# A spectral filter and a sine feed-forward layer on one core: the first batch's backward table, its filter rows and the idle products

## The chip, the core and the metric

The kernel runs on one core of a Trainium2 chip. The core has a matrix engine (TensorE, PE in the profile), a vector engine (VectorE, DVE), a scalar engine (ScalarE, ACT), GpSimd (POOL) and a sync engine (SyncE, SP) that only starts transfers. Each engine works through its own list of instructions in order and waits for the others by semaphores. Transfers between main memory and the on-chip memory run on 16 DMA engines; they are started from the queues of SP, ACT and POOL. TensorE writes its products to PSUM, and VectorE or ScalarE copy them from there to the on-chip memory SBUF. The metric is the time of one execution in microseconds (us) as the device reports it; smaller is better.

## The reference, cut to what matters

```python
batch, seq, dim = (8, 3008, 256)          # d_ff = 2048

def _attn_ref(x, filt_r, filt_i):
    X = np.fft.rfft(x, axis=1)
    F = (filt_r + 1j * filt_i)[None, :, :]
    return np.fft.irfft(X * F, n=x.shape[1], axis=1).astype(np.float32)

def _moe_ref(x, w_in, w_out, alpha):       # x: all 8 * 3008 rows of the above
    h = x @ w_in
    s = np.sin(alpha * h)
    g = h + s * s / (alpha + 1e-09)
    return (g @ w_out).astype(np.float32)
```

Each of 8 batches of 3008 rows of 256 channels goes through a Fourier transform along the rows, a product with a filter per frequency and channel, and the transform back. Then every row goes through a layer of 2048 hidden units with the activation h + sin(alpha h)^2 / alpha.

## The kernel before

**The transform.** 3008 is written as 64 times 47, and 47 x 64 as a two-step transform: a short one of length 47 (24 frequencies are kept, tables `wa`, `wa2` forward and `we`, `we2` backward) and one of length 64 for each of the 24 (tables `wb` forward and `wg` backward, each 128 x 3072 in float16, 786 KB). A tile `xs` holds, for four of the 24, the 128 rows of a spectrum: rows 0 to 63 real parts, 64 to 127 imaginary parts. The filter lies in `fri` (128 x 2 x 24 x 256, real and imaginary plane); its rows 64 to 127 repeat rows 0 to 63, the imaginary plane with its sign changed.

**Batches 1 to 7** store intermediate tiles in main memory and load them back turned (`shuffle1`, `shuffle2`). Their product with the filter (`product`, four VectorE instructions) exchanges the two halves of rows on the way, and one TensorE product with `wg` follows (`f2g`).

**Batch 0** is worked with no such trip. `load_x(0, 4)` loads it in four parts. `f1_chip(k)`, k = 0 to 7, is the short transform (two groups of 4 products, one copied out by ScalarE, one by VectorE, into `a_c`). `turn1(t)`, t = 0 to 11, turns `a_c` by products with the identity into `bint`. `f2x(0, t)` is the long forward transform into `xs`. `product(0, k, 0)` makes z = xs * real filter and t = xs * imaginary filter (the last two on VectorE, 128x1024 each), with no exchange of rows; the exchange is put into a second backward table, `wgs`, which is `wg` with its halves of rows exchanged, so that `g_chip(k, half)` adds two products, z with `wg` and t with `wgs`. `b_c` collects them, `turn2(j)` turns them into `gin[0]` (4 of the 16 turns ahead of the layer, 12 within it), and `f3(G, cb)` is the short transform back into `yt`, the rows that the layer reads. `psf`, the PSUM ring that `turn2` and `f3` share, has three tiles; so has `psh`, which `f1_chip`, `turn1`, `keep_busy` and the layer's first product share; `pso` has two.

Before the change `wgs` is made on the chip: `swap_wg` copies the halves of `wg` (four VectorE copies in all). `fold_filter(s0, n)` fills rows 64 to 127 of `fri` for eight of the 24 frequencies: a VectorE copy for the real plane and a multiplication by -1 for the imaginary one (ScalarE for the first eight, VectorE for the rest). `keep_busy(n, src)` issues n products of 128x512 that nobody reads.

**The layer** goes in 47 groups of 512 rows (index g), each in 8 slots (q): `mlp_in` (two products and one sine on ScalarE, twice a slot), `square` on VectorE every second slot, and `mlp_out` of the group before. A table `plan`, filled by `at(slot, function, ...)`, puts all other work into slot 8g + q: the transforms of the next batch, `prep_w_out` (w_out scaled into `w_out2`), `cast_w_out` (on GpSimd), `prep_w_inT` and `prep_m` (a 256x256 product of the two weights), `prep_w_ina` (w_in times alpha). The program is written under `tc.manual_schedule()`: the order of the instructions on each engine is the order in which the functions are called.

**Queues.** SP carries the tables: `wb` (first 8 frequencies), `wg` (first 8), `wb` (rest), `wg` (rest), then the first half of `w_out`. POOL carries x (batch 0), the filter in twelve transfers, `w_in`, x of batch 1, the second half of `w_out`, `alpha_b` and `w_in32`. `gate` makes a transfer wait for an earlier one to land. The tile pools hand a buffer on when its last reader is done: `wgs` lies in the pool of `vt` before the change.

Of the kernel before, what the change touches and what calls it, by code (L numbers as in the profile page):

```python
# [9 lines left out]
FP16 = mybir.dt.float16  # L10
FP32 = mybir.dt.float32
AFT = mybir.ActivationFunctionType
ALU = mybir.AluOpType

B, S, C, DFF = 8, 3008, 256, 2048
MT, R, NK, RP = 47, 64, 24, 32
# [3 lines left out]
def dft_tables():  # L20

    m = np.arange(MT)
    k1 = np.arange(NK)
    ang = 2 * np.pi * np.outer(m, k1) / MT
    fa = np.concatenate([np.cos(ang), -np.sin(ang)], 1) / np.sqrt(MT)
    wa = np.zeros((MT, 2, 2, 2 * NK))
    wa[:, 0, 0] = fa  # L30
    wa[:, 1, 1] = fa
    wa = wa.reshape(2 * MT, 4 * NK)
    wa2 = wa.reshape(2 * MT, 4, NK).transpose(0, 2, 1).reshape(2 * MT, 4 * NK)

    we = wa.reshape(MT, 2, 4 * NK).transpose(2, 1, 0).reshape(4 * NK, GT)
    we2 = wa2.reshape(MT, 2, 4 * NK).transpose(2, 1, 0).reshape(4 * NK, GT)
    r = np.arange(R)
    wb = np.zeros((2, R, NK, 128))
    wg = np.zeros((128, NK, 2, R))
    q = 1 / np.sqrt(R)  # L40
    d, j, di, ji = slice(0, 32), slice(32, 64), slice(64, 96), slice(96, 128)
    for s in range(NK):
        kd = s + MT * np.arange(32)
        kj = MT * np.arange(1, 33) - s
        td = 2 * np.pi * (np.outer(r, kd) % S) / S
        tj = 2 * np.pi * (np.outer(r, kj) % S) / S
        cd, sd, cj, sj = np.cos(td) * q, np.sin(td) * q, np.cos(tj) * q, np.sin(tj) * q
        wb[0, :, s, d], wb[1, :, s, d], wb[0, :, s, di], wb[1, :, s, di] = (
            cd, sd, -sd, cd)
        wb[0, :, s, j], wb[1, :, s, j], wb[0, :, s, ji], wb[1, :, s, ji] = (  # L50
            cj, -sj, -sj, -cj)
        wd = np.where((kd == 0) | (kd == S // 2), 1.0, 2.0)[:, None]
        wj = np.where(kj == S // 2, 1.0, 0.0 if s == 0 else 2.0)[:, None]
        wg[d, s, 0], wg[di, s, 0], wg[d, s, 1], wg[di, s, 1] = (
            wd * v.T for v in (cd, -sd, sd, cd))
        wg[j, s, 0], wg[ji, s, 0], wg[j, s, 1], wg[ji, s, 1] = (
            wj * v.T for v in (cj, -sj, -sj, -cj))

    wb = wb.reshape(2, 2, RP, NK * 128).transpose(2, 1, 0, 3).reshape(128, NK * 128)
    wg = wg.reshape(128, NK, 2, 2, RP).transpose(0, 1, 4, 3, 2).reshape(128, NK * 128)  # L60
    return [a.astype(np.float16) for a in (wa, wb, wg, we, wa2, we2)]

@with_exitstack
def kernel(
# [10 lines left out]
    nc = tc.nc  # L75
# [3 lines left out]
    def dram(ap, off, dims):  # L79
        return bass.AP(tensor=ap.tensor, offset=ap.offset + off, ap=dims)  # L80

    wa_np, wb_np, wg_np, we_np, wa2_np, we2_np = dft_tables()
    wa_d = nc.inline_tensor(wa_np, name="wa_tbl")
    wb_d = nc.inline_tensor(wb_np, name="wb_tbl")
    wg_d = nc.inline_tensor(wg_np, name="wg_tbl")
    we_d = nc.inline_tensor(we_np, name="we_tbl")
    wa2_d = nc.inline_tensor(wa2_np, name="wa2_tbl")
    we2_d = nc.inline_tensor(we2_np, name="we2_tbl")
    id32_d = nc.inline_tensor(np.eye(16).astype(np.float32), name="id32_tbl")
    id_d = nc.inline_tensor(np.eye(128).astype(np.float16), name="id_tbl")  # L90

    cpool = ctx.enter_context(tc.tile_pool(name="consts", bufs=1))
# [3 lines left out]
    ginpool = ctx.enter_context(tc.tile_pool(name="ginp", bufs=2))  # L96
    ypool = ctx.enter_context(tc.tile_pool(name="yp", bufs=4))
    vpool = ctx.enter_context(tc.tile_pool(name="vp", bufs=2))
# [7 lines left out]
    wa = cpool.tile([GT, 4 * NK], FP16, name="wa")  # L106
    we = cpool.tile([4 * NK, GT], FP16, name="we")
# [13 lines left out]
    def gate(ins, earlier):  # L121

        tc.add_manual_dep(ins.ins, earlier.ins.name, mybir.DependencyInfo(
            mybir.DependencyClass.Sync, mybir.DependencyReason.DATA), reason="order of transfers")
# [122 lines left out]
    def f3(G, cb):  # L247


        b, a = divmod(G, 8)  # L250
        g, lo = divmod(GT * G, 128)
        n = min(GT, 128 - lo)
        if cb == 0:
            if lo == 0 or G == 0:
                yt[g] = ypool.tile([128, 2, 4, 128], FP16, name="yt", tag="yt")
            if n < GT:
                yt[g + 1] = ypool.tile([128, 2, 4, 128], FP16, name="yt", tag="yt")
        ps = psf.tile([128, 4, GT], FP32, name="psy", tag="f")
        for t in range(4):
            nc.tensor.matmul(out=ps[:, t, :], lhsT=gin[b][:, 4 * a + t, 128 * cb:128 * cb + 128],  # L260
                             rhs=we if b else we2, start=True, stop=True)
        nc.scalar.copy(out=yt[g][:, cb, :, lo:lo + n], in_=ps[:, :, 0:n])  # L262
        if n < GT:
            nc.vector.tensor_copy(out=yt[g + 1][:, cb, :, 0:GT - n], in_=ps[:, :, n:GT])  # L264

# [73 lines left out]
    def prep_alpha():  # L339
        ps = pso.tile([128, 2, C], FP32, name="psal", tag="po")  # L340
        nc.tensor.matmul(out=ps[:, 0, 0:16], lhsT=alpha_r, rhs=ident32, start=True, stop=True)
        nc.vector.tensor_copy(out=alpha_t, in_=ps[:, 0, 0:16])
        nc.vector.tensor_scalar(out=recip, in0=alpha_t, scalar1=1e-9, scalar2=None, op0=ALU.add)
        nc.vector.reciprocal(out=recip, in_=recip)
# [47 lines left out]
    def keep_busy(n, src):  # L392

        ps = psh.tile([128, 2, C], FP32, name="idle", tag="ph")
        for _ in range(n):
            nc.tensor.matmul(out=ps, lhsT=ident[0:src.shape[0]], rhs=src, start=True, stop=True)
# [11 lines left out]

    def fold_filter(s0, n):

        nc.vector.tensor_copy(out=fri[64:128, 0, s0:s0 + n, :], in_=fri[0:64, 0, s0:s0 + n, :])
        if s0 == 0:
            nc.scalar.mul(out=fri[64:128, 1, s0:s0 + n, :], in_=fri[0:64, 1, s0:s0 + n, :], mul=-1.0)
        else:
            nc.vector.tensor_scalar(out=fri[64:128, 1, s0:s0 + n, :], in0=fri[0:64, 1, s0:s0 + n, :],
                                    scalar1=-1.0, scalar2=None, op0=ALU.mult)

    def swap_wg(s0, n):

        cs = slice(128 * s0, 128 * s0 + 128 * n)  # L420
        for p in (0, 64):
            nc.vector.tensor_copy(out=wgs[p:p + 64, cs], in_=wg[64 - p:128 - p, cs])

    plan = {}

    def at(slot, f, *args):
        plan.setdefault(int(slot), []).append((f, args))

    for b in range(1, B):
        p = MT * (b - 1)  # L430
# [15 lines left out]
    G = 2  # L446
# [8 lines left out]
    for k in range(2):  # L455
        at(6 + k, prep_w_out, 0, k)
        at(10 + k, prep_w_out, 1, k)
        at(13, prep_m, k)
    at(6, cast_w_out, 0)
    at(7, load_w_out, 1, nc.gpsimd)  # L460
    at(10, cast_w_out, 1)
    at(14, load_w_in32, 0)
# [8 lines left out]
    with tc.manual_schedule():  # L471
# [5 lines left out]
        nc.scalar.dma_start(out=wa, in_=wa_d.ap())  # L477
        nc.scalar.dma_start(out=we, in_=we_d.ap())
        nc.sync.dma_start(out=wb[:, 0:8 * 128], in_=wb_d.ap()[:, 0:8 * 128])
        warm = cpool.tile([128, 1], FP32, name="warm")  # L480
        nc.vector.memset(warm, 0.0)
        nc.scalar.activation(out=warm, in_=warm, func=AFT.Sin)
# [3 lines left out]
        for h in range(2):  # L486
            hs = slice(1024 * h, 1024 * h + 1024)
            for cb in range(2):
                w_in_dma[h, cb] = nc.gpsimd.dma_start(out=w_in16[:, cb, hs],
                                                      in_=moe_w_in[128 * cb:128 * cb + 128, hs])  # L490
        gate(nc.sync.dma_start(out=wg[:, 0:8 * 128], in_=wg_d.ap()[:, 0:8 * 128]), x_dma[0, 2])
        nc.sync.dma_start(out=wb[:, 8 * 128:], in_=wb_d.ap()[:, 8 * 128:])
        gate(nc.sync.dma_start(out=wg[:, 8 * 128:], in_=wg_d.ap()[:, 8 * 128:]), filter_dma[0])
        a_c = vpool.tile([128, 2, NK, 128], FP16, name="a_c", tag="vt")
        prep_alpha()
        for k in range(8):
            f1_chip(k)
            if k == 0:
                keep_busy(3, xt[0][:, 0:2, :])
        bint[0] = xbpool.tile([128, NK, C], FP16, name="bint", tag="xb")  # L500
        wgs = vpool.tile([128, NK * 128], FP16, name="wgs", tag="vt")
        b_c = agpool.tile([128, 2, RP, NK, 4], FP16, name="b_c", tag="ag")
        for t in range(12):
            turn1(t)
            if t in (2, 4, 6, 8, 10, 11):
                f2x(0, (t - 1) // 2)
            if t == 9:
                swap_wg(0, 8)
                fold_filter(0, 8)
        for t in range(16):  # L510
            if t in (4, 8):
                fold_filter(2 * t, 8)
                if t == 4:
                    swap_wg(8, 16)
            if t >= 4:
                g_chip(t // 2 - 2, t % 2)
                if t % 2 and t > 8:
                    keep_busy(2, wg[:, 0:512])
            if 4 <= t < 10:
                f2x(0, t + 2)  # L520
            if t < 12 and t % 2:
                product(0, t // 2, 0)
        gin[0] = ginpool.tile([4 * NK, RP, C], FP16, name="gin", tag="gin")
        for j in range(4):
            turn2(j)
        gate(load_w_out(0, nc.sync), w_in_dma[0, 1])
        load_x(1, 4)
        for i in range(4):
            f3(i // 2, i % 2)

        for g in range(NCH):
            for q in range(8):
# [44 lines left out]
```

## Time and profile before

| what | value |
|---|---|
| median of 3 runs | 839.96 us (838.85 to 840.75) |
| the profiled execution | 839.08 us |
| its span, first to last instruction | 837.3 us |
| outside the span | 1.8 us |
| PE busy | 813.0 us, 97% of the span |
| ACT, DVE, POOL busy | 620.3, 515.2, 36.3 us |
| mean granted TensorE clock | 0.997 of full speed |

The profile is one execution. "Busy" counts an instruction from its start to its end; instructions of one engine can overlap by some 0.1 us, so a duration is a little more than the distance to the next start. In the lists of groups, "idle before" is the time that the engine stood still just ahead of these instructions, with what ended it. In timelines each line is a start, a duration, the engine, the line of the kernel, the operation, the tiles with output before input, the count, and in brackets the idle time ahead. Tables by stretch give the length, then the busy time and the number of instructions of each engine, the granted TensorE clock, the mean busy share of the DMA engines and what they moved. The chain of work follows the time back from the last instruction to what released it each time.

### The profile page before, as it was taken

How to read it: one execution, taken by the hardware profiler on the slowest of the kernel's cores; microseconds unless marked ns; L12 is line 12 of the kernel's file. 1: busy time of each engine (PE TensorE's matmuls, PEld its weight loads, DVE VectorE, ACT ScalarE, POOL GpSimd, SP SyncE). 2: the span in 40 equal slices, each digit the busy share in tenths (PEclk: the TensorE clock that was granted, in tenths of full speed). 3: DMA queues.
4: the chain of work that ended last, by engine and by line, in shares of the span. 5: the costliest groups of instructions: out<-in, count | busy, mean ns of one | idle time of the engine just before them, and what ended most of it. 6: DMA issues, size and time to landing. Idle time of an engine off the chain costs nothing.

```text
span 837.3 us, 15277 instructions
## 1 busy us (share of the span) xinstructions
PE 813.0 (97%) x6221; PEld 573.7 (69%) x6221; DVE 515.2 (62%) x683; ACT 620.3 (74%) x1155; POOL 36.3 (4%) x66
## 2 busy tenths in 40 slices
PE   6779999999999999999999999999999999999997
PEld 5547676677767776677767776677766777767665
DVE  4886975676466665566555684567655675443532
ACT  4786987787777786788777887778877787666662
POOL 5301000000000000000000000000000000000000
PEclk9999999999999999999999999999999999999999
DMA  9926385424644163612834146431645233321122
GB/s 197 208 66 244 103 192 113 139 73 103 152 102 126 51 161 89 201 29 75 196 92 140 51 107 169 103 101 51 160 117 144 61 96 95 61 52 26 28 50 50
DMA packets 68134, 91.55 MB, mean 109 GB/s; under 512 B 7224, under 2 KB 52808, under 8 KB 66552
## 3 DMA queue, kind: packets, MB, share of 16 engines
q1 hardware_dynamic: 61792, 71.25, 30.8%
q0 software_dynamic: 5760, 19.14, 11.2%
q8 instruction: 48, 0.79, 0.4%
q10 hardware_dynamic: 512, 0.19, 0.1%
q14 instruction: 22, 0.18, 0.1%
HBM read 58.83 MB, written 46.66 MB: 126 GB/s over the span
## 4 chain that ended last, share of the span: by engine, by line
PE 90%; DVE 5%; DMA 3%; issue 1%; POOL 1%; ACT 0%; DVEq 0%; POOLq 0%
PE po L290 42%; PE ph L271 37%; PE psa L141 2%; PE psy L260 2%; PE psg L232 2%; PE psx L202 2%; DMA w_out<-in_moe_w_out_dram 1%; DVE vt L278 1%; PE pe L304 1%; DMA fri<-in_filt_i_dram 1%; DMA xt<-in_x_dram 1%; DVE gin L189 1%; DVE w_out L356 1%; PE psg L175 0%; DVE z L215 0%
## 5 line engine op out<-in xcount | busy, mean ns | idle before, releaser
L273 ACT ACTIVATE vt<-ph 128x512 f16<-128x512 f32 x688 | 404.5, 601 | 141.9 <-PE ph L271 136.8
L290 PE MATMUL po<-w_out,vt 128*128 128x256 f16 x2944 | 426.6, 272 | 1.4 <-DVE ot L316 0.8
L290 PEld LDWEIGHTS <-vt 128*128 128x128 f16 x2944 | 287.4, 98 | 173.4 <-issue 2.2
L271 PE MATMUL ph<-yt,w_ina 128*128 128x512 f16 x1376 | 399.3, 379 | 0.0
L278 DVE TENSOR_TENSOR vt<-vt 128x2048 f16<-128x2048 f16 x188 | 230.1, 1224 | 196.6 <-ACT vt L273 196.0
L271 PEld LDWEIGHTS <-w_ina 128*128 128x128 f16 x1376 | 128.2, 98 | 32.8
L316 DVE COPY ot<-po 128x512 f32<-128x512 f32 x92 | 63.0, 688 | 22.4 <-PE po L290 21.4
L206 ACT CAST xs<-psx 128x512 f16<-128x512 f32 x96 | 56.6, 592 | 8.2 <-PE psx L202 8.0
L142 DVE CAST asb<-psa 96x512 f16<-96x512 f32 x56 | 38.2, 685 | 33.4 <-PE psa L141 31.6
L234 ACT CAST gsb<-psg 128x512 f16<-128x512 f32 x84 | 49.5, 589 | 12.3 <-PE psg L232 11.2
L290 PE MATMUL po<-m_t,yt 128*128 128x256 f16 x368 | 55.2, 273 | 0.0
L264 DVE CAST yt<-psy 128x240 f16<-128x240 f32 (+45 forms) x92 | 32.2, 351 | 34.3 <-ACT yt L262 33.3
L262 ACT CAST yt<-psy 128x376 f16<-128x376 f32 (+29 forms) x128 | 46.2, 363 | 7.6 <-PE psy L260 0.7
L273 ACT ACTIVATE vt<-ph,alpha_t 128x512 f16<-128x512 f32 x64 | 42.8, 694 | 11.1 <-PE ph L271 10.8
L260 PE MATMUL psy<-we,gin 96*128 96x94 f16 x512 | 42.1, 204 | 1.1 <-ACT asb L142 0.7
L132 POOL DMA_DIRECT2D xt<-in_x_dram x40 | 20.9, 528 | 496.2 <-PE psy L260 287.5
L260 PEld LDWEIGHTS <-gin 96*128 96x128 f16 x512 | 35.6, 97 | 7.7 <-issue 1.5
L290 PEld LDWEIGHTS <-yt 128*128 128x128 f16 x368 | 36.0, 98 | 4.2
L142 ACT CAST asb<-psa 96x512 f16<-96x512 f32 x56 | 32.3, 583 | 8.0 <-PE psa L141 7.9
L202 PE MATMUL psx<-bint,wb 128*128 128x256 f16 x192 | 37.4, 277 | 0.0
L271 PE MATMUL ph<-yt,w_in 128*128 128x512 f16 x128 | 36.4, 379 | 0.2 <-ACT yt L262 0.2
L215 DVE TENSOR_TENSOR z<-xs,fri 128x1024 f16<-128x1024 f16 x48 | 32.9, 686 | 4.6 <-ACT xs L206 4.5
(71 smaller groups left out, 384.1 us busy)
## 6 DMA issues: line engine op xcount, KB each, us to landing
out_dram<-ot SPq DMA_DIRECT2D x109, 128.0 KB
scr<-asb SPq DMA_DIRECT2D x14, 768.0 KB
bint<-scr SPq DMA_DIRECT2D x21, 512.0 KB
scr<-gsb SPq DMA_DIRECT2D x21, 512.0 KB
xt<-in_x_dram POOLq DMA_DIRECT2D x12, 640.0 KB, 8.1
gin<-scr SPq DMA_DIRECT2D x7, 768.0 KB
out_dram<-ot SPq DMA_DIRECT2D x84, 60.0 KB
gin<-scr SPq DMA_DIRECT2D x7, 576.0 KB
```

The source lines that it names most:

```text
L142: (nc.vector.tensor_copy if u % 2 else nc.scalar.copy)(out=asb[b][:, 2 * u:2 * u + 2, :], in_=ps)
L202: nc.tensor.matmul(out=ps[:, i, :], lhsT=wb[:, 128 * (2 * t + i):128 * (2 * t + i) + 128], rhs=bint[b][:, 2 * t + i, :], start=True, stop= ...
L206: nc.scalar.copy(out=xs[b, t // 2][:, t % 2 * 2:t % 2 * 2 + 2, :], in_=ps)
L215: nc.vector.tensor_tensor(out=z[k], in0=xs[b, k], in1=fri[:, 0, k4, :], op=ALU.mult)
L234: nc.scalar.copy(out=gsb[b][:, 2 * t:2 * t + 2, :], in_=ps)
L260: nc.tensor.matmul(out=ps[:, t, :], lhsT=gin[b][:, 4 * a + t, 128 * cb:128 * cb + 128], rhs=we if b else we2, start=True, stop=True)
L262: nc.scalar.copy(out=yt[g][:, cb, :, lo:lo + n], in_=ps[:, :, 0:n])
L271: nc.tensor.matmul(out=ph, lhsT=(w_in16 if g < 4 else w_ina)[:, cb, 128 * jb:128 * jb + 128], rhs=yt[g][:, cb], start=(cb == 0), stop=(cb ...
L273: nc.scalar.activation(out=vt[g][:, jb, :], in_=ph, func=AFT.Sin, scale=alpha_t[:, jb:jb + 1] if g < 4 else 1.0)
L278: nc.vector.tensor_tensor(out=v4, in0=v4, in1=v4, op=ALU.mult)
L290: nc.tensor.matmul(out=po[g, h][:, i, :], lhsT=vt[g][:, k, ts] if k < 16 else yt[g][:, k - 16, t], rhs=w_out2[:, k, :] if k < 16 else m_t[ ...
L316: nc.vector.tensor_copy(out=ot[g][:, 2 * h:2 * h + 2, :], in_=po[g, h])
```

## The change

A third form of the backward table, with the exchange of halves and the sign in it, is made on the host and loaded: `wgs` = rows 64 to 127 of `wg`, then rows 0 to 63 negated. It takes 786 KB of transfers on the SP queue, in two parts that each follow the same part of `wg`; its buffer now comes from the pool of `gin`. `swap_wg` is gone. `fold_filter` becomes one VectorE copy of both planes (64x4096), unsigned. Since batches 1 to 7 need the sign in `fri`, `negate_filter` multiplies rows 64 to 127 of the imaginary plane by -1 on GpSimd, in three instructions in slots 11, 12 and 13 of the plan. In the built program one more GpSimd instruction stands ahead of the first of them, which the profile calls by its opcode only.

The idle products read a tile of zeros that VectorE sets at the start: 8 ahead of `f1_chip`, 7 within it (before: 3), 4 between `turn1` and `g_chip`, 2 after the `g_chip` of t = 9, 11 and 13 (before also after t = 15). At the end of batch 0's own stage `turn2` and `f3` are interleaved, `load_w_out` and `load_x(1, 4)` come after them, and of the first two blocks' `f3` copies the second half (cb = 1) goes to VectorE.

```diff
+    wgs = np.concatenate([wg[64:], -wg[:64]], 0)
...
-        nc.scalar.copy(out=yt[g][:, cb, :, lo:lo + n], in_=ps[:, :, 0:n])
+        (nc.vector.tensor_copy if G < 2 and cb else nc.scalar.copy)(
+            out=yt[g][:, cb, :, lo:lo + n], in_=ps[:, :, 0:n])
...
     def fold_filter(s0, n):
-        nc.vector.tensor_copy(out=fri[64:128, 0, s0:s0 + n, :], in_=fri[0:64, 0, s0:s0 + n, :])
-        if s0 == 0:
-            nc.scalar.mul(out=fri[64:128, 1, s0:s0 + n, :], in_=fri[0:64, 1, s0:s0 + n, :], mul=-1.0)
-        else:
-            nc.vector.tensor_scalar(out=fri[64:128, 1, s0:s0 + n, :], in0=fri[0:64, 1, s0:s0 + n, :],
-                                    scalar1=-1.0, scalar2=None, op0=ALU.mult)
-    def swap_wg(s0, n):
-        cs = slice(128 * s0, 128 * s0 + 128 * n)
-        for p in (0, 64):
-            nc.vector.tensor_copy(out=wgs[p:p + 64, cs], in_=wg[64 - p:128 - p, cs])
+        nc.vector.tensor_copy(out=fri[64:128, :, s0:s0 + n, :], in_=fri[0:64, :, s0:s0 + n, :])
+
+    def negate_filter(s0, n):
+        nc.gpsimd.tensor_scalar(out=fri[64:128, 1, s0:s0 + n, :], in0=fri[64:128, 1, s0:s0 + n, :],
+                                scalar1=-1.0, scalar2=None, op0=ALU.mult)
...
     at(6, cast_w_out, 0)
+    for k in range(3):
+        at(11 + k, negate_filter, 8 * k, 8)
...
+        zero = cpool.tile([128, 512], FP16, name="zero")
+        nc.vector.memset(zero, 0.0)
...
         gate(nc.sync.dma_start(out=wg[:, 0:8 * 128], in_=wg_d.ap()[:, 0:8 * 128]), x_dma[0, 2])
+        wgs = ginpool.tile([128, NK * 128], FP16, name="wgs", tag="gin")
+        nc.sync.dma_start(out=wgs[:, 0:8 * 128], in_=wgs_d.ap()[:, 0:8 * 128])
         nc.sync.dma_start(out=wb[:, 8 * 128:], in_=wb_d.ap()[:, 8 * 128:])
         gate(nc.sync.dma_start(out=wg[:, 8 * 128:], in_=wg_d.ap()[:, 8 * 128:]), filter_dma[0])
+        nc.sync.dma_start(out=wgs[:, 8 * 128:], in_=wgs_d.ap()[:, 8 * 128:])
         a_c = vpool.tile([128, 2, NK, 128], FP16, name="a_c", tag="vt")
         prep_alpha()
+        keep_busy(8, zero)
         for k in range(8):
             f1_chip(k)
-            if k == 0:
-                keep_busy(3, xt[0][:, 0:2, :])
+            if k in (1, 3, 5, 7):
+                keep_busy(2 if k < 7 else 1, zero)
...
-        wgs = vpool.tile([128, NK * 128], FP16, name="wgs", tag="vt")
...
             if t == 9:
-                swap_wg(0, 8)
                 fold_filter(0, 8)
+        keep_busy(4, zero)
         for t in range(16):
             if t in (4, 8):
                 fold_filter(2 * t, 8)
-                if t == 4:
-                    swap_wg(8, 16)
             if t >= 4:
                 g_chip(t // 2 - 2, t % 2)
-                if t % 2 and t > 8:
-                    keep_busy(2, wg[:, 0:512])
+                if 8 < t < 15 and t % 2:
+                    keep_busy(2, zero)
...
-        for j in range(4):
-            turn2(j)
+        turn2(0)
+        turn2(1)
+        f3(0, 0)
+        f3(0, 1)
+        turn2(2)
+        turn2(3)
+        f3(1, 0)
+        f3(1, 1)
         gate(load_w_out(0, nc.sync), w_in_dma[0, 1])
         load_x(1, 4)
-        for i in range(4):
-            f3(i // 2, i % 2)
```

## The prediction

> **What bounds the kernel now.** I read the table by stretch first. From 300 to 400 us, as everywhere between 200 and 800, TensorE works 100.00 of 100 us at full clock: the layer is TensorE's, and the change adds nothing there. Whatever the first part gains or loses is kept to the end only if it reaches that steady state sooner or later.
>
> ```profile
> 300.00:400.00 100.00, 100.00 (x755) 70.31 (x753) 63.02 (x81) 77.23 (x145) 2.97 (x6) 1.00 0.44 114
> ```
>
> The same table, cut at the stages of the start (columns: stretch, length, PE, PEld, DVE, ACT, POOL, clock, DMA share, GB/s), gives another bound in each.
>
> ```profile
> 19.00:35.00 16.00, 11.53 (x124) 8.96 (x122) 15.43 (x25) 12.76 (x23) 5.45 (x11) 0.89 1.01 215
> 36.60:40.20 3.60, 2.81 (x38) 2.22 (x39) 2.07 (x4) 2.39 (x7) 1.53 (x1) 1.00 1.05 200
> 82.00:102.00 20.00, 19.21 (x147) 13.75 (x146) 19.67 (x29) 18.91 (x35) 0.53 (x1) 1.00 0.37 131
> ```
>
> From 19 to 35 us VectorE is busy 15.43 of 16 us, and the DMA engines are saturated. From 36.6 to 40.2 no engine is full: a chain of short waits. From 82 to 102 VectorE is full again (19.67 of 20), so what holds VectorE there costs one for one; TensorE's one long wait after 70 us is for VectorE's `ot`, 0.8 us near 101. Between, the chain of waits runs through VectorE's `gin` and `vt` to 57 us, then through one transfer:
>
> ```profile
> 37.04 0.59 ACT gin L189
> 38.37 1.11 ACT yt L262 x3
> 39.52 0.59 PE ph L271 x2
> 57.61 8.66 DMA w_out<-in_moe_w_out_dram
> 66.29 2.08 DVE w_out L356
> ```
>
> That transfer starts when VectorE has used the first half of `w_out`, so it moves with everything ahead of it. VectorE's timeline shows what the change removes, and TensorE's what its clock does:
>
> ```profile
> 20.82 0.85 DVE L422 COPY wgs<-wg 64x1024 f16<-64x1024 f16 x2
> 21.60 0.81 DVE L411 COPY fri<-fri 64x2048 f16<-64x2048 f16 x1
> 25.57 0.69 DVE L411 COPY fri<-fri 64x2048 f16<-64x2048 f16 x1
> 26.18 0.68 DVE L415 TENSOR_SCALAR fri<-fri 64x2048 f16<-64x2048 f16 x1
> 26.89 1.39 DVE L422 COPY wgs<-wg 64x2048 f16<-64x2048 f16 x2
> 23.79 0.23 PE L175 MATMUL psg<-wg,z 128*128 128x128 f16 x1 [2.92 <-DVE z L215]
> 25.54 0.31 PE L175 MATMUL psg<-wg,z 128*128 128x128 f16 x1
> 28.01 0.22 PE L175 MATMUL psg<-wgs,t 128*128 128x128 f16 x1
> ```
>
> **The change, part by part** (minus is a gain).
>
> *Idle products ahead of and within `f1_chip`: -1.4 us.* Products of 96 columns start every 0.08 us until 14.4 us (40 in 3.41 us), and 128 columns last 0.31 us at 25.5 but 0.22 at 28.0: TensorE starts at half speed and falls back after the 2.92 us of idleness. The idle products run while TensorE waits for x (until 7.03 us; last part at 12.98) and cost nothing if they end by then: 8 of 0.43 us from 3.8 give 7.2. Warm, the last two `f1_chip` after 12.98 take TensorE 0.32 instead of 0.64 us each, and `turn1` is left to the copies: six on VectorE at 0.62 us until the fold. VectorE reaches the fold at about 15.0 + 0.3 + 3.8 = 19.1 us, not 20.8; I take 1.4 of these 1.7, since the first fold also needs the filter, which came at 18.3 (SP's gated `wg` started at 18.31) and will be later by the table ahead of it. If the clock stays cold, the idle products themselves (up to 7 of 0.43 us between x's parts, 1.1 us of it past x's last part) make it up to 1.3 us later: bounds -1.7 and +1.3.
>
> The row first: granted clock 0.91 at 20 to 25 us and 0.74 at 25 to 30, after that idle gap. The Trainium skill, TensorE: Matmul & The Clock Gate (Part 1: The HAM clock gate), says that about 3.4 us of sustained activity lifts the half-rate state and an idle window of that length restores it; eight idle products of 0.43 us fill such a window, so by that rule the sum is the warm one. It counts activity, not data, as I read it, and no run here yet shows zeros.
>
> *`wgs` no longer copied, the sign gone from the fold: -2.0 us.* VectorE loses 0.85 + 1.39 us of `wgs` copies. The folds took 0.73 + 1.30 + 1.30 on VectorE; one copy of 4096 costs about twice the 0.60 of a 2048 one, 1.2 each, so +0.3. ScalarE loses 1.91 us (L413), not on the chain, as ScalarE is busy 12.76 of 16.
>
> *786 KB more on the SP queue: +0.8 us.* Nothing hides a saturated queue; what counts is what comes late. From 20.5 to 24.7 us the hardware queue moved 0.52 MB (all of `wg`'s second half) and the software queue 0.50 MB:
>
> ```profile
> q0 software_dynamic: 503, 0.50, 72.3%
> q1 hardware_dynamic: 143, 0.52, 41.6%
> ```
>
> `wgs`'s second half follows it. At that rate of 0.125 MB/us it ends 4.2 us after 25.4 (24.7 and 0.7 for the first part's delay), at 29.6; at the 0.23 MB/us that the queue had beside the small filter packets (0.79 MB from 13 to 16.4 us), at 26 to 27. I take 27.5, nearer the second, since the filter is in flight beside it. VectorE would be through its fourth pair of products at 28.3 + 2.4 - 3.4 = 27.3 us; the fifth needs a z buffer that `g_chip` of k = 2 gives back, 1.3 us after `wgs` lands: 28.8, where the fold (1.2) would have let it start at 28.5. The last third of the filter, up to 2 us later than before, holds that fold a further half. Together +0.8; bounds 0 (lands by 27) and +2.4 (lands at 29.6). `w_in` (used at 39.5), `w_out`'s first half (54) and x of batch 1 (48.8) come up to 4 us later and are still early: 0.
>
> *Four idle products more, two less at the end of `g_chip`: 0.* The four stand in the 2.92 us wait. TensorE warm does not speed a stretch that VectorE bounds. The two less are 0.43 us ahead of `turn2`, where TensorE waited for VectorE's `b_c` anyway (36.12 to 36.63).
>
> *`turn2` and `f3` interleaved: +1.5 us.* Before, from `b_c` ready (36.59) to the first sine (40.15) it takes 3.56 us. After, on the same rows: turn2(0) and (1) are copied out by 1.04 (ScalarE) and 1.36 (VectorE); f3(0,0) is made by 1.7 and copied by 2.2, f3(0,1) by 2.45. `psf` has three tiles, so turn2(3) must wait for the copy of f3(0,0): made by 2.6, copied by VectorE (0.69) at 3.35; f3(1,0) at 3.7, its ScalarE copy (0.27) at 4.0. VectorE's copy of that block's rest, 0.36 us, waits for ScalarE (as the row of L264 does before) and stands ahead of its copy for cb = 1: 4.7. Product and sine start: 5.1. Behind it wait `turn2(4)` and all of slot 0. Bounds: +1.6, and -0.6 (two ScalarE copies of 0.3 us off the chain with nothing new in it).
>
> *GpSimd's negations: +0.2 us.* In program order they follow `cast_w_out(1)` (66.3 to 68.2) on POOL, then `alpha_b` (issued at 76.61) and `w_in32`, landing 7.0 us after its issue at 77.15, 84.2; VectorE first uses it at 88.43. POOL thus has 8.4 us before `alpha_b` is late at all, and 4.3 more before VectorE waits: 12.7 us for three negations and the unnamed instruction ahead of them. The nearest row to a negation is POOL's cast, equally 2048 long, 1.90 us: 5.7 in all. The unnamed instruction has no row; the nearest load of an engine's code is ScalarE's table load, 1.28 us. It would have to exceed 7.0 to cost, then one for one. The other price is the port: L356 of 0.34 us took 2.07 while the cast ran.
>
> ```profile
> 66.32 1.90 POOL L352 CAST w_out<-w_out 128x2048 f16<-128x2048 f32 x1 [7.75 <-DMA w_out<-in_moe_w_out_dram]
> L356 DVE TENSOR_SCALAR w_out<-w_out,recip x16: 336/341/2070, 54.2 to 69.9; 128x256 f16<-128x256 f32 x16
> ```
>
> Negations right behind the cast would hold the seven others of that kind, with TensorE behind them; negations from 70 us on meet one `square`, with 0.5 to 0.9 us idle on VectorE around it. Bounds 0 and +4 (three blocks of 1.9, less the 0.88 and 1.01 that VectorE has idle ahead of its rows at 72.8 and 74.3).
>
> The Trainium skill speaks against this part: GPSIMD Engine Reference (section 2.1) puts the first call of freshly loaded code at about 6 us. As an estimate from that page the negations would end 6 + 5.7 us after the cast, inside the 12.7, and the sum stays; no run here shows it.
>
> **Sum:** -1.4 - 2.0 + 0.8 + 1.5 + 0.2 = -0.9 us. The profiled execution took 839.08 (span 837.3, 1.8 around it): 838.2. It lies 0.9 below the median of the runs, 839.96; against that the forecast is 839.1 us, no change that can be told. A measurement of this kernel tells about 0.2%, 1.7 us (its three runs lie 1.9 apart).
>
> **Rivals.**
> *Faster: the table comes in time.* If `wgs`'s second half lands by 27 us, VectorE keeps all 3.4, and if the interleaving costs half of what I count, the sum is -2.5: 837.5. For it: the hardware queue pushed 0.79 MB through in 3.4 us at 13 to 16.4. Against it: 0.125 MB/us at 20.5 to 24.7.
> *Slower: GpSimd late.* The unnamed instruction over 7 us, or negations of over 3 us behind one of 4, holds `alpha_b` and `w_in32`; VectorE stands still before `prep_w_ina` in its full stretch 82 to 102, and `ot` and TensorE behind it. At 3 us over, -1.1 + 3 = +1.9: 841.9. For it: no row bounds that instruction from above. Against: 12.7 us of room.
> *Slower: the clock stays cold*, so the idle products do not do what they are for: -1.4 becomes up to +1.3, the sum +1.8, 841.8. For it: 3.4 us of products over 94 rows between 8.9 and 12.3 did not lift it. Against: it did rise by 17 us among products over 128 rows, and these have 128.
>
> **How the numbers follow.** Forecast (within 0.2%) 0.36; table in time 0.29; GpSimd late 0.17; cold 0.11; port or transfers worse than counted 0.05 (slower), all better 0.02 (faster). So faster 0.31, same 0.36, slower 0.33. The likeliest case alone spans 838.3 to 841.0. The low end goes to 836.5 (-3.4, table in time and interleaving free), the high end to 843.0 (GpSimd late by 4); beyond each lies about a tenth.
>
> **What would show it.** Right: 96-column products at 0.04 us spacing before 13 us; the first fold near 19.5; `g_chip` of k = 2 waiting for a DMA, not for z; over 4.5 us from the last `b_c` copy to the first sine; no VectorE wait at `prep_w_ina`. Wrong: TensorE cold until 17, a fifth pair of products with no wait ahead, a negation or the instruction before it ending after 81 us, or an L356 group with several long members.

## The result

The changed kernel takes 858.16 us (median of 4 runs, 856.87 to 858.78), the kernel before 840.18 beside it (838.85 to 840.75): a ratio of 1.0216, 95% interval 1.0204 to 1.0228. The forecast was 839.1 us, no change that can be told, with 843.0 as its upper end; it was wrong by 19 us. The profiled execution has a span of 855.1 us where before had 837.3.

(Line numbers are those of the changed kernel: the products of `w_out` by `recip`, L356 before, are L359; the casts L355; the negations L417.)

**Where the time went.** TensorE's waits after 30 us (columns: line and releaser, us in total, times, longest) have one new first entry; before, the same wait was 0.6 us:

```profile
PE po L293 <- DVE w_out L359: 11.7, 4, 5.1
PE pst L189 <- DVE gin L191: 1.8, 2, 1.6
```

Before:

```profile
PE po L290 <- DVE w_out L356: 0.6, 1, 0.6
```

The chain of waits passes through the same place. `w_out`'s second half lands 1.9 us later than before; then four products on VectorE take 18.45 us, and TensorE goes on at 86.69, where before it went on at 68.42:

```profile
59.75 8.42 DMA w_out<-in_moe_w_out_dram
68.17 0.02 issue
68.19 18.45 DVE w_out L359 x4
86.65 0.04 issue
86.69 0.80 PE po L293 x3
```

Before:

```profile
68.37 0.04 issue
68.42 0.64 PE po L290 x4
```

GpSimd's timeline shows what ran beside them, and the groups of the two lines (durations min/median/max in ns, then first and last start) show the size of each:

```profile
68.23 1.89 POOL L355 CAST w_out<-w_out 128x2048 f16<-128x2048 f32 x1 [7.51 <-DMA w_out<-in_moe_w_out_dram]
70.22 16.26 POOL L417 TENSOR_SCALAR fri<-fri 64x2048 f16<-64x2048 f16 x3
94.51 0.61 POOL L386 DMA_DIRECT2D alpha_b<-in_moe_alpha_dram  x1 [8.02 <-PE ph L274]
```

```profile
L417 POOL TENSOR_SCALAR fri<-fri x3: 5357/5361/5381, 70.2 to 81.1; 64x2048 f16<-64x2048 f16 x3
L417 POOLq MODIFY_POOL_CONFIG  x2: 8/8/8, 70.1 to 70.1; - x2
```

```profile
L359 DVE TENSOR_SCALAR w_out<-w_out,recip x16: 334/343/5568, 56.4 to 87.3; 128x256 f16<-128x256 f32 x16
```

A negation lasts 5.36 us, not the 1.9 that I took from the cast. Three follow each other right behind the cast, and the eight products of 0.34 us last 19.48 us in all, from 68.19 to 87.7, because one is held by the cast and one by each negation. The unnamed instruction is a setting of 8 ns, and costs nothing.

The table by stretch adds the clock. While TensorE waits, its granted clock falls (0.66 over 68 to 87 us, 1.00 before). From 300 to 400 us nothing is different from before:

```profile
68.00:87.00 19.00, 7.30 (x44) 4.31 (x42) 18.80 (x6) 4.48 (x8) 17.98 (x4) 0.66 0.39 125
300.00:400.00 100.00, 100.00 (x755) 70.37 (x754) 62.49 (x80) 76.86 (x144) 2.07 (x4) 1.00 0.42 111
36.40:43.30 6.90, 6.32 (x39) 4.04 (x39) 3.89 (x9) 2.73 (x5) 0.00 (x0) 0.51 0.95 213
```

**The front part.** Up to the last copy of `b_c` the kernel does what the forecast said: the idle products fill the wait for x, the last `f1_chip` group runs at nearly twice the speed (0.84 us for 16 products, 1.44 before), the first fold stands at 19.83, and `g_chip` waits 1.1 us for the table. TensorE's rows, then VectorE's:

```profile
3.82 3.59 PE L399 MATMUL idle<-zero,ident 128*128 128x512 f16 x8
13.03 0.84 PE L156 MATMUL psa<-wa,xt 94*128 94x96 f16 x16 [0.88 <-DMA xt<-in_x_dram]
```

```profile
19.83 1.22 DVE L414 COPY fri<-fri 64x4096 f16<-64x4096 f16 x1
33.42 0.69 DVE L180 CAST b_c<-psg 128x512 f16<-128x512 f32 x1 [1.45 <-PE psg L177]
```

That last copy stood at 35.89 before: 2.47 us are gained between these two executions. But the first sine comes only at 39.65 (40.15 before), since the stretch from `b_c` to it has grown from 3.57 to 5.54 us. VectorE's and ScalarE's rows of it before, then ScalarE's and VectorE's after:

```profile
35.89 0.69 DVE L178 CAST b_c<-psg 128x512 f16<-128x512 f32 x1 [1.23 <-PE psg L175]
40.15 0.69 ACT L273 ACTIVATE vt<-ph,alpha_t 128x512 f16<-128x512 f32 x1 [0.51 <-PE ph L271]
```

```profile
36.23 0.58 ACT L191 CAST gin<-pst 96x512 f16<-96x512 f32 x1
38.05 0.27 ACT L264 CAST yt<-psy 128x136 f16<-128x136 f32 x1 [1.24 <-PE psy L262]
39.65 0.69 ACT L276 ACTIVATE vt<-ph,alpha_t 128x512 f16<-128x512 f32 x1 [1.32 <-PE ph L274]
```

```profile
36.93 0.69 DVE L191 CAST gin<-pst 96x512 f16<-96x512 f32 x1 [0.38 <-PE pst L189]
38.35 0.41 DVE L267 CAST yt<-psy 128x240 f16<-128x240 f32 x1 [0.74 <-ACT yt L264]
38.68 0.29 DVE L264 CAST yt<-psy 128x136 f16<-128x136 f32 x1
```

And TensorE's clock is low there (0.51 from 36.4 to 43.3 in the table above). From the first sine to the issue of `w_out`'s second transfer it takes 20.1 us (39.65 to 59.75), where before it took 17.5 (40.15 to 57.61), so that transfer is issued 2.1 us later than before. The loss of 17.8 us of span thus has two parts: 1.9 to 2.1 that are there when `w_out` lands, and about 16 behind it.

### The profile page after: what moved, and what is told of

Its sections match the earlier page's. It is cut to its first block, busy times and chain, and to the rows that moved or that the text cites. A ratio compares the mean times of both kernels' runs of the same rounds, so it can differ in the third digit from the quotient of the medians.

```text
span 855.1 us, 15303 instructions
## 1 busy us (share of the span) xinstructions
PE 821.2 (96%) x6235; PEld 574.7 (67%) x6235; DVE 530.7 (62%) x680; ACT 617.3 (72%) x1152; POOL 53.2 (6%) x69
## 3 DMA queue, kind: packets, MB, share of 16 engines
q0 software_dynamic: 5760, 19.14, 10.9%
## 4 chain that ended last, share of the span: by engine, by line
PE 88%; DVE 5%; DMA 4%; issue 2%; POOL 0%; ACT 0%; SPq 0%; POOLq 0%
PE po L293 41%; PE ph L274 36%; PE psa L143 2%; PE psy L262 2%; DVE w_out L359 2%; PE psg L234 2%; PE psx L204 2%; DMA w_out<-in_moe_w_out_dram 1%; DMA fri<-in_filt_i_dram 1%; DMA wgs<-wgs_tbl 1%; PE pe L307 1%; DMA xt<-in_x_dram 1%; DVE vt L281 1%; PE psm L379 0%; PE psg L177 0%
## 5 line engine op out<-in xcount | busy, mean ns | idle before, releaser
L264 ACT CAST yt<-psy 128x376 f16<-128x376 f32 (+45 forms) x126 | 45.7, 363 | 10.6 <-PE psy L262 3.7
L274 PE MATMUL ph<-yt,w_in 128*128 128x512 f16 x128 | 39.3, 402 | 0.1
```

The costliest lines, as they stand in the source:

```text
L264: (nc.vector.tensor_copy if G < 2 and cb else nc.scalar.copy)(out=yt[g][:, cb, :, lo:lo + n], in_=ps[:, :, 0:n])
L274: nc.tensor.matmul(out=ph, lhsT=(w_in16 if g < 4 else w_ina)[:, cb, 128 * jb:128 * jb + 128], rhs=yt[g][:, cb], start=(cb == 0), stop=(cb ...
```

## The experiments

Theory P: a GpSimd instruction holds VectorE's work from SBUF to SBUF beside it; the negations stand where the most urgent of that work stands. The rivals: the front part and its clock carry the loss (F, C); GpSimd's late queue does; the extra work does, on whatever engine.

### The negations left out

```
-    for k in range(3):
-        at(11 + k, negate_filter, 8 * k, 8)
```

> The changed kernel with GpSimd's three negations left out (so the folded imaginary filter rows keep the wrong sign for batches 1 to 7). Theory P (port: a GpSimd negation holds every VectorE instruction that reads and writes SBUF beside it): the eight products by recip behind the cast go back to 0.34 us each, TensorE waits about 0.5 us for them instead of 11.7, and the time falls by the 16.2 us that appear there, to about 842. Rival C (the clock: TensorE idles because its front part came late, and the cold clock after it costs most): only the wait's cause goes, the 2 us of lateness stay and the clock goes cold again near 68: 848 to 853. Rival F (the front part, the table and the interleaving carry the loss): 857 to 858.

Measured: 841.74 us (839.17 to 843.49, 10 runs), ratio to before 1.0025 (1.0015 to 1.0035). The products and TensorE's wait for them are back to what they were before:

```profile
L359 DVE TENSOR_SCALAR w_out<-w_out,recip x16: 340/342/2069, 56.3 to 71.7; 128x256 f16<-128x256 f32 x16
```

```profile
PE po L293 <- DVE w_out L359: 0.4, 1, 0.4
```

The negations cost 16.4 us (858.16 less 841.74; 16.0 by the two ratios to before). What is left, 2.1 us, belongs to the front part. Its runs lie 4.3 us apart, where before's lie 1.6 apart.

### The negations on VectorE

```
-        nc.gpsimd.tensor_scalar(out=fri[64:128, 1, s0:s0 + n, :], in0=fri[64:128, 1, s0:s0 + n, :],
+        nc.vector.tensor_scalar(out=fri[64:128, 1, s0:s0 + n, :], in0=fri[64:128, 1, s0:s0 + n, :],
```

> The three negations in the same slots, on VectorE instead of GpSimd (complete computation). Theory P: they are VectorE's own 0.6 us each beside no GpSimd work, 1.9 us in all, of which VectorE's idle time there hides part: 842 to 844. A rival by which the extra work itself, on whatever engine, is what TensorE waits for: 855 or more.

Measured: 841.83 us (839.12 to 843.00), ratio 1.0024 (1.0013 to 1.0035): the same as without them. The work is free on VectorE, so it is not its amount that costs.

### The negations alone, in the kernel before

```
+    def negate_filter(s0, n):
+        nc.gpsimd.tensor_scalar(out=fri[64:128, 1, s0:s0 + n, :], in0=fri[64:128, 1, s0:s0 + n, :],
+                                scalar1=-1.0, scalar2=None, op0=ALU.mult)
...
+    for k in range(3):
+        at(11 + k, negate_filter, 8 * k, 8)
```

> The kernel before with one part of the change alone: three GpSimd negations of the same blocks in the same slots (their sign is thereby turned twice, for batches 1 to 7). Theory P: eight products by recip at 66.3 us meet cast and negations, as after: TensorE's start after them slips by 15 to 16.5 us: 855 to 857. Rival F or C: 840 to 846, since the front part is that of before and its clock is warm.

Measured: 855.94 us (855.27 to 856.64), ratio 1.0195 (1.0180 to 1.0210): 16.5 us from this part alone, with the front part of before. TensorE's wait is the one of the changed kernel:

```profile
PE po L290 <- DVE w_out L356: 11.6, 4, 5.1
```

F and C, as causes of the large loss, fall.

### The negations on GpSimd, but in slot 0

```
     for k in range(3):
-        at(11 + k, negate_filter, 8 * k, 8)
+        at(0, negate_filter, 8 * k, 8)
```

> The three negations stay on GpSimd but are issued in slot 0, right behind batch 1's x (about 39.5 to 55.6 us), so cast and products by recip at 68 us meet none. VectorE's work there reads PSUM, but for a square every 4 to 5 us. Theory P: 5.4 us each again; two or three squares last until a negation ends (2 to 5 us instead of 1.2 to 1.4), the first cast slips to 57.5 and w_out's second half by about 1 us: 843 to 848. A rival by which GpSimd's late order (negations ahead of alpha_b and w_in32) is the cause: 842. A rival by which each negation costs its length wherever it stands: 858.

Measured: 842.88 us (840.23 to 846.24), ratio 1.0039 (1.0022 to 1.0056), 1.1 above the kernel without negations, which the two intervals do not tell from nothing. They last as long here, from 34.74 to 51.0, and cost next to nothing: neither their length nor GpSimd's time is enough to cost, it matters what stands beside them. Two squares, VectorE's only work from SBUF in that time, lie inside the second and the third negation, and were held less than P said. The third negation and the squares:

```profile
45.65 5.36 POOL L417 TENSOR_SCALAR fri<-fri 64x2048 f16<-64x2048 f16 x1
```

```profile
44.25 1.23 DVE L281 TENSOR_TENSOR vt<-vt 128x2048 f16<-128x2048 f16 x1
48.30 2.06 DVE L281 TENSOR_TENSOR vt<-vt 128x2048 f16<-128x2048 f16 x1 [0.43 <-ACT vt L276]
```

The square at 44.25 was not held at all. So P as I had put it, for any work from SBUF, was not the whole of it; the next experiment looks at the form of the instruction.

### The products in the two-input form

```
-            nc.vector.tensor_scalar(out=w_out2[:, 8 * h + i, :], in0=w_out32[h][:, i, :],
-                                    scalar1=recip[:, 8 * h + i:8 * h + i + 1], scalar2=None,
-                                    op0=ALU.mult)
+            nc.vector.tensor_tensor(out=w_out2[:, 8 * h + i, :], in0=w_out32[h][:, i, :],
+                                    in1=recip[:, 8 * h + i:8 * h + i + 1].to_broadcast([128, C]),
+                                    op=ALU.mult)
```

> The changed kernel, GpSimd's negations in their place, but the products of w_out by recip as VectorE's two-input form (recip spread over the row) instead of the form with a scalar per partition. Theory P1 (a GpSimd negation holds VectorE's SBUF work of any form): three products of about 5.5 us again, 857 to 859. Theory P2 (it holds the form with one input, not the two-input form: at slot 0 two squares inside negations of 5.36 us took 1.23 and 2.06): the first may still wait for the cast (2.1 us), the others last 0.3 to 0.8 us: TensorE waits under 3 us for them, 842 to 845.

Measured: 847.30 us (846.48 to 848.76), ratio 1.0092 (1.0077 to 1.0107): between the two theories, 10.9 below the changed kernel and above P2's 845. One product is held by the cast (2.11 us), the next lasts 3.86 us beside the first negation, and then five more pass beside that negation; two squares are held later. The group of the products, two of the negations, and the squares beside them:

```profile
L359 DVE TENSOR_TENSOR w_out<-w_out,recip x16: 409/412/3860, 55.8 to 75.1; 128x256 f16<-128x256 f32 x16
```

```profile
75.34 5.37 POOL L417 TENSOR_SCALAR fri<-fri 64x2048 f16<-64x2048 f16 x1
80.79 5.36 POOL L417 TENSOR_SCALAR fri<-fri 64x2048 f16<-64x2048 f16 x1
```

```profile
76.01 4.05 DVE L281 TENSOR_TENSOR vt<-vt 128x2048 f16<-128x2048 f16 x1
81.15 4.35 DVE L281 TENSOR_TENSOR vt<-vt 128x2048 f16<-128x2048 f16 x1
```

GpSimd is late here as well: `w_in32` is issued only behind the negations, at 86.82, and VectorE waits 3.08 us for it. That is the mechanism of the prediction's rival "GpSimd late", and may be a part of the 5.6 us that this kernel takes above the one without negations:

```profile
96.50 0.69 DVE L392 TENSOR_TENSOR w_ina<-w_in,alpha_b 128x512 f16<-128x512 f32 x1 [3.08 <-DMA w_in<-in_moe_w_in_dram]
```

A square that waited for the cast (in the kernel without negations: cast 43.73 to 45.62, square to 46.70) ends 1.08 us after the cast, which I take as its release. Taken off here, the squares were released at 78.98 and 84.42, which is 3.64 and 3.63 us after the negations' starts; the square of the slot-0 kernel at 49.28, again 3.63 after 45.65; and that kernel's other square began 4.0 us into its negation and ran free. The held product gives 3.68 in the same way (the product that the cast held ended 0.27 after the cast). So a negation holds the two-input form for about the first 3.63 of its 5.36 us, and the one-input form with a scalar to its end: the second product of the changed kernel, from 70.19, ended 5.57 us later, 0.15 after the first negation's end.

The Trainium skill, SBUF — State Buffer (Who interferes with whom), says that GpSimd and VectorE share one pair of ports, locked for a whole instruction. By it VectorE's fast one-input forms contend for both ports, and a two-input form with GpSimd's reads alone. That both forms are held agrees with it; that a two-input form stays blocked until the GpSimd instruction ends, as the page also has it, these runs do not show: it was let go after 3.63 us of 5.36.

### Copies in place of the negations

```
-        nc.gpsimd.tensor_scalar(out=fri[64:128, 1, s0:s0 + n, :], in0=fri[64:128, 1, s0:s0 + n, :],
-                                scalar1=-1.0, scalar2=None, op0=ALU.mult)
+        nc.gpsimd.tensor_copy(out=fri[64:128, 1, s0:s0 + n, :], in_=fri[64:128, 1, s0:s0 + n, :])
```

> The changed kernel with GpSimd copying the three blocks onto themselves instead of negating them (sign left out for batches 1 to 7). If a copy takes 1.9 us, as the cast of equal length, and holds one product each: three products of about 2 us, and the time is the 841.7 without negations plus 3 to 4.5: 845 to 846, the prediction's upper bound for this term. If the length is that of 16-bit data or of work in place, whatever the operation: 5.4 us each, 857 to 859.

Measured: 846.12 us (845.62 to 846.76), ratio 1.0076 (1.0062 to 1.0090). The groups of GpSimd's copies and of the products:

```profile
L417 POOL COPY fri<-fri x3: 1893/1953/1955, 71.4 to 75.2; 64x2048 f16<-64x2048 f16 x3
```

```profile
L359 DVE TENSOR_SCALAR w_out<-w_out,recip x16: 336/343/2068, 57.5 to 78.0; 128x256 f16<-128x256 f32 x16
```

The same blocks, type and place, but 1.9 us each: the length is that of the operation, not of the data. The 16.4 us split into 4.4 that three blocks of the length I had assumed cost in this place, and 12.0 for their being 5.36 us long (three times 3.41, 10.2, is length alone; beside the remaining 1.8 stands TensorE's clock, which falls there with the negations and in this kernel's profiled execution does not; that it makes up the 1.8 was not tried).

### The front part: order, idle products

Two kernels undo the interleaving, two add idle products to TensorE's waits there; all have the negations on VectorE. The order undone, ahead of the first slot (the `f3` copies go back to ScalarE too):

```
-        turn2(0)
-        turn2(1)
-        f3(0, 0)
-        f3(0, 1)
-        turn2(2)
-        turn2(3)
-        f3(1, 0)
-        f3(1, 1)
+        for j in range(4):
+            turn2(j)
         gate(load_w_out(0, nc.sync), w_in_dma[0, 1])
         load_x(1, 4)
+        for i in range(4):
+            f3(i // 2, i % 2)
```

> Negations on VectorE, and the interleaving of turn2 and f3 undone (four turn2, then f3, all four f3 copies on ScalarE, as before). Theory I (the interleaving gives back the front part's gain): from b_c's last copy to the first sine about 3.6 us instead of 5.5 to 6.2, the first sine near 37.5: 839.5 to 840.2, 1.6 to 2.3 below the same kernel with interleaving (841.8). Theory K (the gain is lost to TensorE's cold clock between 36 and 43 us, where it has few products, whatever their order): the first sine comes earlier, but the clock still falls in most executions: 840.5 to 842, with the same spread of 4 us.

The order kept, with idle products:

```
+        keep_busy(2, zero)
         turn2(0)
         turn2(1)
+        keep_busy(2, zero)
...
         turn2(3)
+        keep_busy(2, zero)
         f3(1, 0)
         f3(1, 1)
+        keep_busy(1, zero)
```

> Negations on VectorE, interleaving kept, and seven idle products put into TensorE's waits from the last g_chip to the first mlp_in. Theory K: the clock stays at 1.00 from 31 to 50 us, the spread of the runs falls from 4 to about 1.5 us, and the median falls to 839.5 (the best of the runs without it was 839.1). Theory I: nothing is gained, the idle products add up to 1 us to the chain: 841.5 to 843.

Both (two idle products ahead of `turn2`, two after its third, two after the second `f3`, one after the last):

> Both: interleaving undone, and idle products in the waits there. If I and K both hold and add: 837.0 to 838.5, below the kernel before by 1 to 2.5. If I alone holds: as with the order undone alone, up to 1 more. If K alone holds: as with the idle products alone.

Measured: order undone 838.02 us (836.49 to 840.55), ratio 0.9982 (0.9973 to 0.9991); idle products 839.23 (838.22 to 840.88), 0.9995 (0.9987 to 1.0004); both 838.29 (837.01 to 838.94), 0.9980 (0.9971 to 0.9989). Against the kernel with the negations on VectorE (1.0024) the order, with the engine of the copies and the place of the two loads, brings 0.42%, 3.5 us, the idle products alone 2.4, and both no more than the order alone.

The stretch itself is read at a full clock, in the two kernels with these idle products: interleaved, from `b_c`'s last copy (35.67 and 36.12 on the two engines, the later ending at 36.81) to the first sine at 41.90, 5.09 us; undone, 33.90 to 37.53, 3.63 us. ScalarE's sine with the order kept, then VectorE's `b_c` copy and ScalarE's sine with the order undone:

```profile
41.90 0.69 ACT L276 ACTIVATE vt<-ph,alpha_t 128x512 f16<-128x512 f32 x1 [1.11 <-DMA xt<-in_x_dram]
```

```profile
33.21 0.69 DVE L180 CAST b_c<-psg 128x512 f16<-128x512 f32 x1 [1.25 <-PE psg L177]
37.53 0.69 ACT L275 ACTIVATE vt<-ph,alpha_t 128x512 f16<-128x512 f32 x1 [0.51 <-PE ph L273]
```

So I holds: the interleaving costs 1.46 us by itself (1.3 by the times of these two kernels). The idle products do not make the difference: with the clock full, the stretch is 5.09 also in the interleaved kernel with the two-input products, and 3.57 in the one with only the order undone.

K is shown in part. With the idle products the runs lie 2.7 us apart instead of 3.9, and in the profiled execution the clock was full in the stretch where it was 0.51:

```profile
36.40:43.30 6.90, 5.81 (x58) 3.48 (x58) 4.44 (x9) 2.81 (x6) 2.19 (x2) 1.00 1.06 212
```

From the first sine to the issue of `w_out`'s second transfer it then took 17.5 us, as before, and not 20.1. But in this execution the clock had fallen earlier (0.86 over 24 to 36 us), and `b_c` ended at 36.81, where it ended at 34.11 in the changed kernel. The kernel with the two-input products kept its clock in the later stretch with no idle product in it, after an early fall as well. That the 2.4 us come from the clock is therefore argued, from one execution of each kernel.

An early fall is not free either. With the order undone the clock was 0.86 over 24 to 36 us and `b_c` ended at 36.43; with both it was 1.00 and `b_c` ended at 33.90. These two executions took 839.18 and 837.01 us, though the medians of the two kernels do not differ.

### Idle products alone, the table alone

In the kernel before, first the idle products:

```
         prep_alpha()
+        keep_busy(8, zero)
         for k in range(8):
             f1_chip(k)
-            if k == 0:
-                keep_busy(3, xt[0][:, 0:2, :])
+            if k in (1, 3, 5, 7):
+                keep_busy(2 if k < 7 else 1, zero)
...
+        keep_busy(4, zero)
         for t in range(16):
             if t in (4, 8):
```

> The kernel before with the idle products alone (eight ahead of f1_chip, seven within it, four ahead of the first g_chip; none taken away). The prediction's term: the clock rises near 9 instead of 17 us, the first fold comes 1.0 to 1.4 us earlier, and all behind it: 838.1. If what arrives by transfer (the filter, wg) sets the pace instead, or the clock falls later on: 839.0 to 840.

and then the table:

```
+    wgs = np.concatenate([wg[64:], wg[:64]], 0)
...
+        wgs = ginpool.tile([128, NK * 128], FP16, name="wgs", tag="gin")
+        nc.sync.dma_start(out=wgs[:, 0:8 * 128], in_=wgs_d.ap()[:, 0:8 * 128])
...
+        nc.sync.dma_start(out=wgs[:, 8 * 128:], in_=wgs_d.ap()[:, 8 * 128:])
...
-                swap_wg(0, 8)
...
-                if t == 4:
-                    swap_wg(8, 16)
```

> The kernel before with the exchanged table loaded instead of copied on VectorE (without signs, since the folds of that kernel turn them), and nothing else. The prediction's terms: 2.24 us of VectorE copies go, at most 0.8 to 2.4 come back through the queue: 837.5 to 839.5 with the middle at 838.4. With idle products alone the gain was 0.97, with all of the front part, idle products and VectorE negations 1.85, so by sums the table and the folds bring 0.9: 838.9. If the queue delays wb, wg or the filter by more than VectorE gains: 840 or more.

Measured: idle products 838.90 us (838.25 to 839.83), 0.97 below before, ratio 0.9991 (0.9982 to 0.9999); the table 838.37 (837.38 to 840.42), 1.57 below, ratio 0.9983 (0.9973 to 0.9992). The kernel with both, the plain folds, the negations on VectorE and the order undone gained 1.85, less than the 2.5 of the two together, but within the noise of the three medians. In its profiled execution VectorE waits 0.16 us for the filter's last block before the third fold at 29.01; whether transfers are the next limit was not tried.

### The cast after the products

On the kernel with the order undone and idle products in `turn2` and `f3`, GpSimd's second cast waits for VectorE's last product (and is issued in slot 11, not 10):

```
     def cast_w_out(h):
-        nc.gpsimd.tensor_copy(out=w_out16[:, 8 * h:8 * h + 8, :], in_=w_out32[h])
+        ins = nc.gpsimd.tensor_copy(out=w_out16[:, 8 * h:8 * h + 8, :], in_=w_out32[h])
+        if h:
+            gate(ins, last_prep[0])
```

> The best so far (838.3: order undone, idle products, negations on VectorE) with GpSimd's second cast made to wait for VectorE's last product by recip, so that the cast's 1.89 us hold none of them. If that hold (first product 2.07 us instead of 0.34) is on the chain: TensorE's wait there of 0.5 us goes and VectorE is through 1.7 us earlier: 837.3 to 838.0. If VectorE or TensorE makes it up before 100 us: 838.0 to 838.6.

Measured: 837.39 us (836.68 to 839.45, 10 runs), ratio to before 0.9974 (0.9965 to 0.9983), the fastest of all kernels here. No product is held any more (longest 354 ns, 2069 without the gate):

```profile
L362 DVE TENSOR_SCALAR w_out<-w_out,recip x16: 341/346/354, 54.3 to 68.3; 128x256 f16<-128x256 f32 x16
```

Whether that itself brings time is not settled: 0.9974 and the 0.9980 without it lie within each other's intervals.

## Why the prediction was wrong

**GpSimd's negations, +0.2 us (bounds 0 and +4): measured +16.4. This step failed**, in two ways.

First its place. The text named the price ("negations right behind the cast would hold the seven others of that kind, with TensorE behind them") and then took the case "from 70 us on", where they meet one `square`. But the rows of before shown in it put the cast's end at 66.32 + 1.90 = 68.22, the products' end at 69.9 + 0.34, and nothing on GpSimd's queue between cast and negations: the named case was the one that the rows gave. Copies of the assumed 1.9 us cost 4.4 in that place, not 0.2: the upper bound of 4, within the noise of the two medians.

Second its size. The cast was the only row of GpSimd's arithmetic and I took its rate for another operation: 5.36 us against 1.9. The text did think of negations of over 3 us, but only for GpSimd's queue; the upper bound of the hold kept the 1.9. Together with a hold that scales with the length, this was the larger part, 12.0 us.

**The unnamed instruction**, on which a rival of 17 in 100 stood: the profile lists it twice, 8 ns each. The 6 us that the Trainium skill, GPSIMD Engine Reference (section 2.1), gives for a first call of freshly loaded code do not appear in this trace: the first negation starts 0.12 us after the second of these rows and, with 5.38 us, is 0.02 longer than the others. Whether any code was loaded here, the trace does not say. `alpha_b` was issued at 94.51, long after the negations' end at 86.5, behind TensorE: GpSimd was not late in this kernel. The loss had been given a place in the case "port or transfers worse than counted", with 5 in 100.

**Idle products, -1.4:** -0.97 alone. The mechanism is as described: the granted clock rose 9.15 us into the changed kernel instead of at 17.3, and in the kernel with the negations on VectorE at 6.87, when only products of zeros had run for 3 us and the first product of x was still to come (7.39; its first 16 take 0.84 us, in the changed kernel 1.44). So products of zeros count as activity, as the prediction had read the Trainium skill, TensorE: Matmul & The Clock Gate (Part 1). **Table and folds with the queue's price, -2.0 + 0.8 = -1.2:** the table alone -1.57, where its own terms gave -2.24 + 0.8 = -1.4. The table landed at 27.74 (27.5 forecast) and made `g_chip` wait, as said. In the trace the three terms together, -2.6 forecast, are -2.47 at the last copy of `b_c`; in the time, with the order undone, 1.85. The -2.47 has luck in it. Ten profiled executions here have this front part: in five the clock did not fall ahead of that copy, and it ended at 33.9 to 34.4 us; in five it did, and the copy ended at 35.8 to 36.8. Before had 36.58, and its clock had fallen too: the -2.47 compares an execution without a fall with one that has it.

**Interleaving, +1.5:** 1.46 at a full clock; right in size and in mechanism (the `psf` tile, VectorE's copy of the rest behind ScalarE's). What the step missed is that the clock can fall at 36.5 us, in the stretch where TensorE feeds the first sines; the text had looked for a cold clock only ahead of the fold. Seven idle products in that stretch bring 2.4 us in the median. The front part is +2.1 instead of the -1.1 of the forecast's own sum without the negations.

**The rivals:** "table in time" did not happen (27.74, 1.1 us of waiting); "clock stays cold" did not, in the place that it named; "GpSimd late" did not, by its mechanism, in the changed kernel; with the two-input products it did. Of the signs that the text gave for being wrong, the profile shows two: an L356 group with several long members, and a negation that ends after 81 us (86.49).

## What to carry to other kernels

Work moved to an idle GpSimd is priced by what VectorE does at the same moment, not by GpSimd's own time: the same 16 us of negations cost 16.4 us behind the cast, and in slot 0 at most a little (1.1, within the noise). Ask what runs on GpSimd's queue at the instant when a landing transfer releases VectorE's urgent work, and give an operation without a row a slow rate as its upper bound. Where a chain of short waits grows, look at TensorE's clock there too: seven idle products brought back 2.4 us.

## What the runs showed of the hardware

- GpSimd's multiplication by a constant on 64 x 2048 fp16 values takes 5.36 us, a copy of the same block 1.95, a cast of 128 x 2048 fp32 values 1.89.
- While the negation runs, VectorE's form with one input and a scalar, SBUF to SBUF, is held to its end (5.52 to 5.57 us for 0.34 of work); the form with two inputs is held for its first 3.63 us (three squares, within 0.01; a product gave 3.68) and then runs at full speed beside it. The cast held the two-input form to its own end (in three kernels the square ended 1.08 us after the cast). Copies from PSUM were not held: in slot 0 VectorE's stayed at 0.68 us beside the negations.
- Three negations in a row held three products of the one-input form, one each: the held product ended 0.15 us after its negation, and the next product had by then met the next negation. In the trace the held products begin 0.01 to 0.04 us ahead of the negations that hold them.
- Eight products of zeros from 3.8 us lifted TensorE's clock, in one execution at 6.87 us, ahead of any product of x. In 13 of the 14 profiled executions, that of the kernel before among them, it fell to half again somewhere between 20 and 46 us, for 3.4 or 6.8 us at a time. The runs of the interleaved kernels without idle products in that stretch and without the hold lie 4 to 6 us apart, where before's lie within 2.6.
